# Row maxima of an attention kernel: one shared tile for a pair of heads, one scores tile per unit of work

## The chip, the cores and the metric

The kernel runs on one core of a Trainium2 chip. The metric is the device time of one launch in microseconds, as a median of runs. The core has a matrix engine (TensorE, PE in the profile), a vector engine (VectorE, DVE), a scalar engine (ScalarE, ACT), a general engine (GpSimd, POOL), and a synchronising engine (SyncE, SP) that here issues nearly all DMAs. Each engine works through its own instruction list in order and waits on semaphores for the others.

## The reference

Attention with a threshold, followed by two feed-forward layers. Per batch (4) and head (8), with 576 rows and a head size of 64, in float32:

```python
scores = scale * q @ k.T
thresh = max(scores, axis=-1) - tau
scores = where(scores >= thresh, scores, -1e9)
attn = exp(scores - max(scores)); attn /= sum(attn) + 1e-9
x = attn @ v                       # -> 2304 x 512
x = g(x @ w_in) @ w_out            # 512 -> 2048 -> 512, g piecewise quadratic
x = layernorm(solu(x @ w_in2)) * g_ln @ w_out2   # 512 -> 1024 -> 512
```

The change lies in the attention alone.

## The kernel before

Attention runs over 16 pairs of heads. A pair has nine units of work (`UNITS`), 144 in all. A unit covers 128 keys of one head, except the pair's fifth: 576 is four and a half times 128, so it covers the last 64 keys of the even head and the first 64 of the odd one. For these the keys of the even head lie in columns 0 to 575 of its tiles and those of the odd head in columns 64 to 639 (`key_off`), with zeros in the other 64 columns, so that both heads add up in one tile of scores.

A unit makes the scores with keys on the partitions and queries along the columns, already shifted by the row maximum (`shifted`, tile zt, line 378); ScalarE takes the exponential (`expo`, line 389); VectorE sets to zero what is below the threshold (`mask`, line 394). One unit later `p_split` makes a rounded high half on ScalarE (phi, line 402) and the remainder on GpSimd (plo, line 403), because the matrix engine works in a shortened float32 and each product is made of a high and a low part. Three units later `values` multiplies by v (tile av, line 426), and `store_head` copies a finished head out (xs, line 438).

The shift must be known before a head's first unit. So `scores` makes a head's scores once more ahead of time, with queries on the partitions (tile sc, line 305): five tiles a head, the fifth with only 64 rows in use. `row_max` reduces each (mcol, line 318, VectorE). `row_shift` (ScalarE and GpSimd) turns the five columns into a shift in two parts, `shift_turn` transposes it on TensorE (tile tm, line 339), and `shift_store` copies it (mt, line 345) and writes it by a DMA issued from ScalarE into two rows of q_m (line 346), which the shifted scores read. All this is done once per head.

Before that, `load_kq` loads q and k of a pair by eight DMAs, `transpose_kq` turns them (tr, line 262), `split_kq` makes high (q_st, line 270) and low (lo, line 271) parts, and `stack_k` and `stack_q` copy pieces between partitions by DMA: k_both from q_st (line 285) and from lo (286), q_m from q_st (289), q_st from lo (293). The last one overwrites the rows that the first one reads. SyncE issues all of these, and also the loads of v, the stores of finished heads (lines 440, 441) and the raw weights.

The order on each engine is written by hand. `attention_unit(u)` goes through a string `ORDER[u % 9]`, one letter after another: S one tile of scores, x one row maximum, F the splitting of q and k, E shifted scores and exponential, M mask, v and V the values matmuls, p the split of unit u-1, L the store of a head, P transposes on TensorE, A row shift, shift store and split of v, T the SyncE work, J a step of the weight decoding. The constants give the unit, counted from the pair's first, at which a thing is done: `T_A`, `T_B` the transposes of the even and odd head (stacking one and three units later, the load five units before `T_A`), `S_UNITS` the ten scores tiles, `TURN_AT` the transpose of the shift, `V_AT` the split of v. `T_FIRST`, `T_SECOND` are those of the first two pairs, and `U0` the first unit. Scores, shifted scores and both kinds of transposes share three PSUM buffers (`ps_r`) in the order in which they are issued.

During attention twelve blocks of weights are decoded from 64-bit words by `Jobs`, a new one every `JOB_EVERY` units; `DECODE` says in which unit which kind of step may be done. A step's five VectorE operations are in lines 487 to 500.

## Time and profile before

| | us |
|---|---|
| median of 3 runs (lowest, highest) | 1044.88 (1042.83, 1046.16) |
| the profiled execution's own time | 1043.3 |
| its span, first to last instruction | 1041.5 |
| TensorE busy | 969.5 (93%) |
| VectorE busy | 732.1 (70%) |
| GpSimd busy | 598.0 (57%) |
| ScalarE busy | 535.3 (51%) |

The busy share of TensorE counts a matmul from its start to its modelled end, and successive matmuls overlap; 93% is therefore not a share of its peak. Attention takes about the first 405 us, and the two feed-forward layers the rest.

### The profile page before, as it was taken

How to read it: one execution, taken by the hardware profiler on the slowest of the kernel's cores; microseconds unless marked ns; L12 is line 12 of the kernel's file. 1: busy time of each engine (PE TensorE's matmuls, PEld its weight loads, DVE VectorE, ACT ScalarE, POOL GpSimd, SP SyncE). 2: the span in 40 equal slices, each digit the busy share in tenths (PEclk: the TensorE clock that was granted, in tenths of full speed). 3: DMA queues.
4: the chain of work that ended last, by engine and by line, in shares of the span. 5: the costliest groups of instructions: out<-in, count | busy, mean ns of one | idle time of the engine just before them, and what ended most of it. 6: DMA issues, size and time to landing. Idle time of an engine off the chain costs nothing.

```text
span 1041.5 us, 15175 instructions
## 1 busy us (share of the span) xinstructions
PE 969.5 (93%) x5232; PEld 841.7 (81%) x5232; DVE 732.1 (70%) x1133; ACT 535.3 (51%) x1006; POOL 598.0 (57%) x569
## 2 busy tenths in 40 slices
PE   4899899889979998999999999999999999999998
PEld 3788888788878897767887888788888988888886
DVE  3788888868877775588747875787567556666662
ACT  2666666756756666645443443444344534344433
POOL 6577778967786776657524552555256823344332
PEclk9999999989999999999999999999999999999999
DMA  6555556555755520321121112111211104444443
GB/s 155 136 136 135 124 136 160 136 122 131 184 145 126 132 70 24 91 84 59 33 71 61 42 41 81 51 51 41 91 41 51 56 7 132 108 121 127 122 131 91
DMA packets 89885, 99.89 MB, mean 96 GB/s; under 512 B 50032, under 2 KB 62640, under 8 KB 89808
## 3 DMA queue, kind: packets, MB, share of 16 engines
q1 hardware_dynamic: 89424, 98.76, 36.5%
q8 instruction: 41, 0.67, 0.3%
q14 instruction: 36, 0.29, 0.1%
q10 hardware_dynamic: 384, 0.16, 0.1%
HBM read 55.13 MB, written 15.88 MB: 68 GB/s over the span
## 4 chain that ended last, share of the span: by engine, by line
PE 54%; issue 13%; DVE 12%; POOL 10%; ACT 6%; DMA 3%; SPq 2%; ACTq 0%; POOLq 0%; DVEq 0%
PE y L779 10%; PE h L742 10%; PE o L932 10%; PE h L821 9%; PE av L426 6%; PE zt L378 5%; PE sc L305 3%; DVE e L394 3%; POOL gl L763 3%; POOL dec_a L504 2%; POOL plo L403 2%; POOL wg L533 2%; ACT e L389 2%; DVE mcol L318 2%; DMA q_st<-lo 1%
## 5 line engine op out<-in xcount | busy, mean ns | idle before, releaser
L403 POOL TENSOR_TENSOR plo<-e,phi 128x576 fp32r<-128x576 f32 x144 | 206.2, 1438 | 80.7 <-ACT phi L402 79.5
L763 POOL TENSOR_TENSOR gl<-cl,gh 128x512 fp32r<-128x512 f32 (+1 forms) x80 | 96.9, 1211 | 189.4 <-ACT gh L762 156.0
L779 PE MATMUL y<-gh,wg 128*128 128x512 f32 (+1 forms) x640 | 187.6, 374 | 4.1 <-ACT gh L762 4.1
L742 PE MATMUL h<-xh,wg 128*128 128x512 f32 (+1 forms) x640 | 185.8, 371 | 2.0 <-DVE e L394 2.0
L394 DVE SCALAR_TENSOR_TENSOR e<-zt,ntau,e 128x576 f32<-128x576 f32 x144 | 116.6, 810 | 64.9 <-ACT e L389 64.7
L758 ACT ACTIVATE h<-h,mone 128x512 f32<-128x512 f32 (+1 forms) x80 | 49.5, 619 | 198.8 <-DVE cl L757 198.6
L389 ACT ACTIVATE e<-zt 128x576 f32<-128x576 f32 x144 | 93.7, 651 | 96.6 <-PE zt L378 81.1
L779 PEld LDWEIGHTS y<-gh,wg 128*128 128x128 f32 x640 | 117.9, 188 | 24.1 <-ACT gh L762 7.8
L742 PEld LDWEIGHTS h<-xh,wg 128*128 128x128 f32 x640 | 119.0, 189 | 19.2 <-DVE e L394 2.3
L779 PE MATMUL y<-gl,wg 128*128 128x512 f32 (+1 forms) x320 | 122.0, 381 | 10.2 <-POOL gl L763 10.2
L318 DVE TENSOR_REDUCE mcol<-sc 128x1 f32<-128x576 f32 x160 | 116.7, 747 | 10.4 <-PE sc L305 10.4
L757 DVE TENSOR_SCALAR cl<-h 128x512 f32<-128x512 f32 (+1 forms) x80 | 50.8, 635 | 102.0 <-PE h L742 69.0
L742 PE MATMUL h<-xl,wg 128*128 128x512 f32 (+1 forms) x320 | 118.8, 371 | 0.0
L932 PE MATMUL o<-wg,ln 128*128 128x512 f32 x432 | 103.2, 395 | 0.0
L821 PE MATMUL h<-wg,y 128*128 128x512 f32 x432 | 101.2, 390 | 0.0
L402 ACT CAST phi<-e 128x576 fp32r<-128x576 f32 x144 | 96.3, 669 | 2.1 <-DVE e L394 1.9
L932 PEld LDWEIGHTS o<-wg,ln 128*128 128x128 f32 x432 | 81.0, 188 | 19.2
L821 PEld LDWEIGHTS h<-wg,y 128*128 128x128 f32 x432 | 81.0, 188 | 17.0
L896 POOL TENSOR_TENSOR ln<-land,ln 128x1024 fp32r<-128x1024 f32 x16 | 38.5, 2408 | 92.2 <-ACT ln L895 86.4
L378 PE MATMUL zt<-q_st,k_both 128*128 128x288 f32 x320 | 76.9, 322 | 10.4 <-ACT mt L345 5.2
L305 PE MATMUL sc<-k_both,q_st 128*128 128x288 f32 x320 | 73.4, 312 | 13.1 <-DMA q_st<-lo 8.7
L779 PEld LDWEIGHTS y<-gl,wg 128*128 128x128 f32 x320 | 60.1, 188 | 27.3 <-POOL gl L763 19.1
(109 smaller groups left out, 1940.4 us busy)
## 6 DMA issues: line engine op xcount, KB each, us to landing
raw<-in_moe_w_in_dram SPq DMA_DIRECT2D x24, 512.0 KB
raw<-in_moe_w_out_dram SPq DMA_DIRECT2D x24, 512.0 KB
k_both<-q_st SPq DMA_DIRECT2D x30, 288.0 KB
sq<-so SPq DMA_DIRECT2D x64, 128.0 KB
land<-sq SPq DMA_DIRECT2D x16, 512.0 KB
k_both<-lo SPq DMA_DIRECT2D x32, 144.0 KB
q_st<-lo SPq DMA_DIRECT2D x32, 144.0 KB
x<-xs SPq DMA_DIRECT2D x32, 144.0 KB
```

Source lines behind the costliest of these rows:

```text
L305: nc.tensor.matmul(ps[:, c, 0:HS], lhsT=st[j][i][r, n * P : n * P + P], rhs=kk[j][i][r, o + c * HS : o + (c + 1) * HS], start=(st is q_st) ...
L318: nc.vector.tensor_reduce(mc[:, n : n + 1], sc_ps.pop((h, n))[:, :, 0:HS], axis=AXES.XY, op=ALU.max, negate=True)
L378: nc.tensor.matmul(ps[:, c, 0:HS], lhsT=st, rhs=mv[:, c * HS : (c + 1) * HS], start=(m == 0), stop=(m == len(todo) - 1),)
L389: nc.scalar.activation(out=e, in_=st_ps[u][:, :, 0:HS], func=ACTF.Exp)
L394: nc.vector.scalar_tensor_tensor(out=e, in0=st_ps.pop(u)[:, :, 0:HS], scalar=ntau[:, 0:1], in1=e, op0=ALU.is_ge, op1=ALU.mult)
L402: nc.scalar.copy(hi, e)
L403: (nc.vector if u - NU in LO_DVE or u < NU - UNITS and u % UNITS in LO_UNITS else nc.gpsimd).tensor_tensor(lo, e, f32(hi), op=ALU.subtract)
L742: nc.tensor.matmul(ps, lhsT=a[:, kk, f], rhs=m[:, kk, :], start=(n == 0 and kk == 0), stop=(n == 2 and kk == KD - 1),)
L763: nc.gpsimd.tensor_tensor(gl, cl, f32(gh), op=ALU.subtract)
L779: nc.tensor.matmul(y_ps[c][d], lhsT=a[:, jj, ds_], rhs=m, start=(jj == 0 and n == 0), stop=(jj == JG - 1 and n == 2),)
L821: nc.tensor.matmul(ps[g], lhsT=a[:, kk, :], rhs=wg_t["in2", g][s][:, kk, :], start=(n < 2), stop=(n >= 6 * KD - 2),)
L932: nc.tensor.matmul(ps, lhsT=a[:, f, :], rhs=wg_t["out2", f // 4][m][:, f % 4, :], start=(n == 0), stop=(n == len(terms) - 1))
```

## The change

The odd head's queries now lie in columns 64 to 639 of q_st and q_m, as its keys do, so the fifth scores tile of a pair holds the last 64 queries of the even head and the first 64 of the odd one, with eight matmuls that add up in one tile. A pair has nine scores tiles instead of ten, in the order 0, 1, 2, 3, 5, 4, 6, 7, 8, one per unit from unit -14 to unit -6. The column of maxima of the shared tile is copied once on GpSimd, since both heads need it. Row shift, transpose and copy are done once for the pair (for the first pair still once per head); the two DMAs into q_m remain. One string gives the order of every unit. The transposes stand 6 units earlier (with the loads, five units before), the odd heads' tiles have three buffers instead of two, jobs come every 10 units, v is split at unit -2, and the tiles e, phi, plo, xs and mt each have one buffer fewer.

```diff
-    T_A, T_B = -16, -10
-    S_UNITS = (-10, -9, -7, -7, -6, -5, -4, -3, -3, -2)
+    T_A, T_B = -22, -16
+    S_FIRST = -14
...
-    JOB_EVERY = 9
...
-    ORDER = (
-        "FESvSxvMxxpVPLTASJ",
-        "vFEvSSTSxxMxxxpLVPAJ",
-        "EvvvSSSMxxxVLFPATpJ",
-        "FESvSSxxMxxpVLPATJ",
-        "FESSSMJvxxxpVLPAT",
-        "FEvvSSSMxxxpVLPATJ",
-        "FvJEvSSSMxxxpVLPAT",
-        "FEvvvSSSMxxxVLPvATpJ",
-        "FSEvPSSTMxxxpVLAJ",
-    )
+    JOB_EVERY = 10
...
+    ORDER = "SxFEvMvpVLPATJ"
...
-    V_AT = -5
+    V_AT = -2
...
-    LO_UNITS = ()
...
-    LO_DVE = ()
...
-    T_SECOND = (-13, -2)
+    T_SECOND = (-13, -7)
...
-    DECODE = ('', '', 's', 'asb', '', 's', '', 'as', 'asb')
+    DECODE = ('asb', 's', 'asb', 'a', 'sb', 'asb', 'a', 's', 'asb')
...
-    NBUF = (3, 2)
+    NBUF = (3, 3)
...
     def key_off(h):
...
+    def on(h):
+        return slice(64 * (h % 2), 64 * (h % 2) + S)
...
     def buf(h):
...
-                nc.gpsimd.memset(f32(q_st[j][i][:, S:SP]), 0.0)
-                nc.gpsimd.memset(f32(q_m[j][i][0:D, S:SP]), 0.0)
+                nc.gpsimd.memset(f32(q_st[j][i][:, pad]), 0.0)
+                nc.gpsimd.memset(f32(q_m[j][i][0:D, pad]), 0.0)
...
         for t in v_nat if first else ():
...
-        hi = q_st[j][i][:, 0:S]
+        hi = q_st[j][i][:, on(h)]
...
     def stack_k(h):
...
-        kh = f32(q_st[j][i][0:D, 0:S])
-        o = slice(key_off(h), key_off(h) + S)
+        o = on(h)
+        kh, qh = f32(q_st[j][i][0:D, o]), f32(q_st[j][i][D:P, o])
...
-            nc.scalar.copy(q_m[j][i][0:D, 0:S], f32(q_st[j][i][D:P, 0:S]))
+            nc.scalar.copy(q_m[j][i][0:D, o], qh)
...
-        if h < FAST:
-            return
-        nc.sync.dma_start(f32(q_m[j][i][0:D, 0:S]), f32(q_st[j][i][D:P, 0:S]))
+        if h >= FAST:
+            nc.sync.dma_start(f32(q_m[j][i][0:D, o]), qh)
...
     def stack_q(h):
...
-        nc.sync.dma_start(f32(q_st[j][i][0:D, 0:S]), f32(tr_t.pop(h)[D:P, :]))
+        nc.sync.dma_start(f32(q_st[j][i][0:D, on(h)]), f32(tr_t.pop(h)[D:P, :]))
...
-    def scores(h, n):
-        j, i = buf(h)
-        o = key_off(h)
...
+    S_ORDER = (0, 1, 2, 3, 5, 4, 6, 7, 8)
...
+    def scores(p, n):
...
-        for st, kk in ((q_st, k_st), (q_m, k_on)):
-            r = slice(0, P if st is q_st else R1)
+        todo = []
+        for h in ([2 * p] if n <= 4 else []) + ([2 * p + 1] if n >= 4 else []):
+            j, i = buf(h)
+            at_ = slice((n - 4 * j) * P, (n - 4 * j) * P + P)
+            for st, kk, r in ((q_st, k_st, P), (q_m, k_on, R1)):
+                todo.append((st[j][i][0:r, at_], kk[j][i][0:r, on(h)]))
+        for m, (st, mv) in enumerate(todo):
             for c in range(2):
...
-                    lhsT=st[j][i][r, n * P : n * P + P],
-                    rhs=kk[j][i][r, o + c * HS : o + (c + 1) * HS],
-                    start=(st is q_st),
-                    stop=(st is q_m),
+                    lhsT=st,
+                    rhs=mv[:, c * HS : (c + 1) * HS],
+                    start=(m == 0),
+                    stop=(m == len(todo) - 1),
...
-        sc_ps[h, n] = ps
...
-    def row_max(h, n):
-        if n == 0:
-            mcol[h] = att_p.tile([P, NTI], F32, tag="mcol", name="mcol", bufs=2)
-        mc = mcol[h]
+        sc_ps[p, n] = ps
...
+    def row_max(p, n):
+        if p not in mcol:
+            mcol[p] = att_p.tile([P, 2, NTI], F32, tag="mcol", name="mcol", bufs=2)
+        mc = mcol[p].rearrange("p j n -> p (j n)")
+        m = n + (n > 4)
...
-            mc[:, n : n + 1], sc_ps.pop((h, n))[:, :, 0:HS], axis=AXES.XY, op=ALU.max, negate=True
+            mc[:, m : m + 1], sc_ps.pop((p, n))[:, :, 0:HS], axis=AXES.XY, op=ALU.max, negate=True
...
-    def row_shift(h):
-        mc = mcol.pop(h)
...
-        sh = att_p.tile([P, 2, NTI], F32, tag="sh", name="sh", bufs=2)
-        mr = att_p.tile([P, 2, NTI], F32R, tag="mr", name="mr", bufs=2)
-        nc.scalar.activation(out=sh[:, 0, :], in_=mc, func=ACTF.Abs, scale=DELTA)
-        nc.scalar.activation(out=sh[:, 1, :], in_=sh[:, 0, :], func=ACTF.Relu, bias=ntau[:, 0:1], scale=1.0)
-        nc.gpsimd.tensor_tensor(sh[:, 0, :], sh[:, 1, :], mc, op=ALU.add)
-        nc.gpsimd.tensor_copy(mr[:, 0, :], sh[:, 0, :])
-        nc.gpsimd.tensor_tensor(mr[:, 1, :], sh[:, 0, :], f32(mr[:, 0, :]), op=ALU.subtract)
-        mr_t[h] = mr
+        if n == 4:
+            nc.gpsimd.tensor_copy(mc[:, 5:6], mc[:, 4:5])
...
-    def shift_turn(h):
+    def row_shift(p, js):
...
+        mc = mcol[p][:, js, :]
...
+        sh = att_p.tile([P, 2, 2, NTI], F32, tag="sh", name="sh", bufs=2)
+        mr = att_p.tile([P, 2, 2, NTI], F32R, tag="mr", name="mr", bufs=2)
+        s0, s1, m0, m1 = sh[:, 0, js], sh[:, 1, js], mr[:, js, 0, :], mr[:, js, 1, :]
+        nc.scalar.activation(out=s0, in_=mc, func=ACTF.Abs, scale=DELTA)
+        nc.scalar.activation(out=s1, in_=s0, func=ACTF.Relu, bias=ntau[:, 0:1], scale=1.0)
+        nc.gpsimd.tensor_tensor(s0, s1, mc, op=ALU.add)
+        nc.gpsimd.tensor_copy(m0, s0)
+        nc.gpsimd.tensor_tensor(m1, s0, f32(m0), op=ALU.subtract)
+        mr_t[p, js.start] = mr[:, js]
...
+    def shift_turn(p, js):
...
-        nc.tensor.transpose(ps[0 : 2 * NTI, 0:P], f32(mr_t.pop(h)).rearrange("p l n -> p (l n)"), ident)
-        mr_t[h] = ps
...
-    def shift_store(h):
-        j, i = buf(h)
-        mt = att_p.tile([2 * NTI, P], F32R, tag="mt", name="mt", bufs=2)
-        nc.scalar.copy(mt, mr_t.pop(h)[0 : 2 * NTI, 0:P])
-        nc.scalar.dma_start(f32(q_m[j][i][R1:R3, :]), f32(mt))
+        mr = f32(mr_t.pop((p, js.start))).rearrange("p j l n -> p (j l n)")
+        nc.tensor.transpose(ps[0 : mr.shape[1], 0:P], mr, ident)
+        mr_t[p, js.start] = ps[0 : mr.shape[1], 0:P]
...
+    def shift_store(p, js):
+        mt = att_p.tile([4 * NTI, P], F32R, tag="mt", name="mt", bufs=1)
+        ps = mr_t.pop((p, js.start))
+        nc.scalar.copy(mt[0 : ps.shape[0]], ps)
+        for n, h in enumerate(range(2 * p + js.start, 2 * p + js.stop)):
+            j, i = buf(h)
+            nc.scalar.dma_start(f32(q_m[j][i][R1:R3, :]), f32(mt[2 * NTI * n : 2 * NTI * n + 2 * NTI, :]))
...
-            todo += [(k_st[j][i][:, cols], q_st[j][i]), (k_on[j][i][:, cols], q_m[j][i])]
+            todo += [(k_st[j][i][:, cols], q_st[j][i][:, on(h)]), (k_on[j][i][:, cols], q_m[j][i][:, on(h)])]
         for m, (st, mv) in enumerate(todo):
             for c in range(2):
...
     def expo(u):
-        e = att_p.tile([P, 2, HS], F32, tag="e", name="e", bufs=4)
+        e = att_p.tile([P, 2, HS], F32, tag="e", name="e", bufs=3)
...
     def p_split(u):
...
-        hi = att_p.tile([P, 2, HS], F32R, tag="phi", name="phi", bufs=5)
-        lo = att_p.tile([P, 2, HS], F32R, tag="plo", name="plo", bufs=5)
+        hi = att_p.tile([P, 2, HS], F32R, tag="phi", name="phi", bufs=4)
+        lo = att_p.tile([P, 2, HS], F32R, tag="plo", name="plo", bufs=4)
...
-        (nc.vector if u - NU in LO_DVE or u < NU - UNITS and u % UNITS in LO_UNITS else nc.gpsimd).tensor_tensor(lo, e, f32(hi), op=ALU.subtract)
+        nc.gpsimd.tensor_tensor(lo, e, f32(hi), op=ALU.subtract)
...
     def store_head(h):
...
-            xs = att_p.tile([P, 2, HS], F32, tag="xs", name="xs", bufs=2)
+            xs = att_p.tile([P, 2, HS], F32, tag="xs", name="xs", bufs=1)
...
     for p in range(NP):
-        for n, d in enumerate(S_UNITS):
-            at(s_at, UNITS * p + d, None, 2 * p + n // NTI, n % NTI)
-        for j in range(2):
-            t = UNITS * p + S_UNITS[NTI * j + NTI - 1]
-            at(act_, t + 1, row_shift, 2 * p + j)
-            at(pe_, t + TURN_AT, shift_turn, 2 * p + j)
-            at(act_, t + TURN_AT, shift_store, 2 * p + j)
+        for k_, n in enumerate(S_ORDER):
+            at(s_at, UNITS * p + S_FIRST + k_, None, p, n)
+        for js, last in ((slice(0, 1), 4), (slice(1, 2), 8)) if p == 0 else ((slice(0, 2), 8),):
+            t = UNITS * p + S_FIRST + S_ORDER.index(last)
+            at(act_, t + 1, row_shift, p, js)
+            at(pe_, t + TURN_AT, shift_turn, p, js)
+            at(act_, t + TURN_AT, shift_store, p, js)
...
     def attention_unit(u):
...
         for w, j in ((u - LAGV - 1, 1), (u - LAGV, 0), (u - LAGV, 1)):
...
-        for what in ORDER[u % UNITS]:
+        for what in ORDER:
...
```

## Rows read from the trace of the kernel before

**Rows 1.** Busy time by window: length, each engine (instructions), granted clock, DMA.

```profile
147.30:171.40 24.10, 21.95 (x153) 20.15 (x154) 21.17 (x29) 16.28 (x31) 18.63 (x19) 1.00 0.62 154
195.40:225.00 29.60, 24.37 (x153) 22.28 (x153) 19.69 (x27) 16.52 (x31) 21.40 (x21) 0.88 0.63 155
296.70:325.10 28.40, 23.30 (x153) 21.49 (x152) 19.78 (x27) 16.00 (x30) 19.87 (x20) 0.94 0.65 156
347.90:370.30 22.40, 21.17 (x154) 19.98 (x153) 16.57 (x24) 15.20 (x29) 15.37 (x16) 1.00 0.47 108
```

**Rows 2.** Instruction groups 110 to 330 us, VectorE: busy us, mean ns.

```profile
L318 DVE TENSOR_REDUCE mcol<-sc 128x1 f32<-128x576 f32 x87 | 63.5, 745 | 7.8 <-PE sc L305 7.8
...
L271 DVE SCALAR_TENSOR_TENSOR lo<-tr,scale,q_st 128x576 fp32r<-128x576 f32 x17 | 13.7, 805 | 0.0
L493 DVE SCALAR_TENSOR_TENSOR dec_a<-raw,dec_a 128x512 uint32<-128x512 uint32 x9 | 12.7, 1411 | 0.0
L490 DVE TENSOR_SCALAR dec_a<-dec_a 128x512 uint32<-128x512 uint32 x9 | 12.5, 1390 | 0.0
...
L487 DVE TENSOR_SCALAR dec_a<-dec_a 128x512 f32<-128x512 f32 x9 | 8.5, 949 | 0.0
...
L500 DVE SCALAR_TENSOR_TENSOR raw<-raw 128x512 f32<-128x512 uint32 x9 | 8.2, 911 | 0.0
...
L497 DVE TENSOR_SCALAR raw<-dec_a 128x512 uint32<-128x512 uint32 x8 | 6.6, 827 | 0.0
```

**Rows 3.** Timeline around 163 us: start, length, instruction, idle before.

```profile
163.09 0.43 PE L305 MATMUL sc<-k_both,q_m 65*128 65x288 f32 x2
...
163.36 0.43 PE L426 MATMUL av<-plo,v_hi 128*128 128x288 f32 x2
...
164.52 0.27 PE L339 MATMUL tm<-ident,mr 128*10 128x128 f32 x1 [0.73 <-DVE e L394]
164.83 0.26 ACT L345 CAST mt<-tm 10x128 fp32r<-10x128 f32 x1 [1.40 <-PE tm L339]
...
165.13 0.52 PE L378 MATMUL zt<-q_st,k_both 128*128 128x288 f32 x2 [0.34 <-ACT mt L345]
```

**Rows 4.** Timeline around 152 us, ScalarE and its DMA queue.

```profile
151.82 0.62 ACTq L346 DMA_DIRECT2D q_m<-mt  x1
...
152.54 0.65 ACT L389 ACTIVATE e<-zt 128x576 f32<-128x576 f32 x1 [0.75 <-PE av L426]
```

**Rows 5.** Chain of waits in the two stalls and at the start: start, length.

```profile
199.83 6.12 DMA k_both<-q_st
...
205.97 3.76 DMA q_st<-lo
...
301.38 5.58 DMA k_both<-q_st
...
15.47 2.73 DMA q_st<-lo
```

**Rows 6.** Timeline of the start, TensorE, SyncE and ScalarE.

```profile
13.35 1.38 PE L262 MATMUL tr<-ident,nat 128*128 128x128 f32 x5 [3.90 <-DMA nat<-in_k_dram]
...
18.33 0.82 PE L305 MATMUL sc<-k_both,q_st 128*128 128x288 f32 x2 [3.60 <-DMA q_st<-lo]
...
23.84 1.26 SPq L219 DMA_DIRECT2D nat<-in_q_dram  x2
...
27.79 1.25 SPq L229 DMA_DIRECT2D nat<-in_k_dram  x2
...
29.13 0.64 SPq L285 DMA_DIRECT2D k_both<-q_st  x1
...
29.63 0.65 ACT L389 ACTIVATE e<-zt 128x576 f32<-128x576 f32 x1 [0.48 <-PE zt L378]
```

**Rows 7.** Instruction groups 147.3 to 171.4 us, GpSimd.

```profile
L403 POOL TENSOR_TENSOR plo<-e,phi 128x576 fp32r<-128x576 f32 x10 | 14.2, 1422 | 4.5 <-ACT phi L402 4.5
L253 POOL TENSOR_TENSOR v_lo<-v_nat,v_hi 128x640 fp32r<-128x640 f32 x1 | 1.6, 1579 | 0.0
```

## The prediction

> **What bounds the kernel now.** I read the busy table by stage first. Attention fills the first 405 us or so, and the change touches nothing after it. In a steady stretch of 24.1 us, TensorE (PE) has 153 matmuls and is busy 21.95 us, VectorE (DVE) 21.17, GpSimd (POOL) 18.63 and ScalarE (ACT) 16.28 [rows 1]. One pair of heads needs 152 matmuls (40 of scores, 40 of shifted scores, 60 of values, 10 transposes of q and k, 2 of row maxima), so 24.1 us is the price of a pair while weights are being decoded; after the decoding it is 22.4 us. No engine is full, so next I read the timeline. Two matmuls of 288 columns follow two others after 0.27 us [rows 3]: 0.134 us each, or 20.4 us for 152. The other 3.7 us of a pair are holes, and one hole is in these rows: the last values matmul is issued by 163.63, the transpose of the maxima waits for a score buffer until 164.52, ScalarE copies it out from 164.83, and the next shifted scores start at 165.13. That is 1.5 us. Three buffers of PSUM circulate among scores, shifted scores and transposes, so a tile waits for the third before it to be released.
>
> The third view is the chain of waits. Two stretches carry one pair's matmuls but take 29.6 and 28.4 us instead of 24.1, with the granted clock down to 0.88 and 0.94 [rows 1]. In the first the chain runs through two DMAs in a row: the stacking copy of the k half from 199.83, which takes 6.12 us, and then the copy of the q remainder, 3.76 us [rows 5]. The second may not be issued before the first is through, because it overwrites what the first reads. TensorE can't begin the odd head's scores before both have landed. The second stretch shows the same copy, 5.58 us long.
>
> **The change part by part.**
> *The middle tile.* Per pair the scores are 8 tiles of four matmuls and one of eight: 40 matmuls, as before. TensorE gains nothing but one small transpose of the maxima, 0.27 us of latency and about 0.13 of issue. VectorE loses one reduction of 0.745 us per pair [rows 2]. The row shift runs once instead of twice (two short ScalarE and three short GpSimd instructions fewer, one short GpSimd copy more); it is off the path because both engines have over 5 us free per pair [rows 1].
>
> *The jobs.* A weight block has five VectorE steps: 0.949 + 1.390 + 1.411 + 0.827 + 0.911 = 5.49 us [rows 2]. One per 10 units instead of 9 takes 0.55 us from a pair, and the jobs last 11 units longer, which returns it; I count it at zero. VectorE's load per pair is then 21.17 - 0.75 - 0.55 = 19.9 us, just under TensorE's 20.3.
>
> *One order for all units.* This should set the pace. A unit now has one scores tile, then one shifted tile; before, some units issue two scores tiles together, with the transpose of the maxima right behind them and ahead of the shifted scores. With one scores tile ahead of every shifted tile, the transpose (letter P, at the end of the unit) takes the buffer of the shifted tile of the unit before, whose mask is long done. So the 1.5 us hole goes. The holes at the transposes of q and k I leave: the shifted tile after one still takes the buffer of the last shifted tile. The gain is bounded by 0 (new holes of the same size) and by 24.1 - 20.5 = 3.6 us a pair (a full TensorE). I take the row that I can see, 1.5 us, for the 13 pairs that run with scores all along: -19.5 us.
>
> *Earlier transposes and a third buffer for odd heads.* From a head's stacking to its first scores there were five units for an even head and four for an odd one (from -15 to -10, from -9 to -5); now there are seven and six (from -21 to -14, from -15 to -9). At 2.5 us a unit the odd head's 10 us become 15. The chain that stalled took 199.83 to 209.73, 9.9 us [rows 5], so 15 us covers it. The stalls go: (29.6 - 24.1) + (28.4 - 24.1) = 9.8 us. Next late is SyncE's queue, which issues all of these copies in order. Bounds: 0, if a queue that falls behind uses up the lead, to -9.8. I take -9.8, because the lead grows by more than the 4 us hole.
>
> *The start.* Here the change costs, since moved instructions move past each other on SyncE's queue. Before, head 3 (the odd head of the second pair) is transposed 2 units before unit 0, and the load of q and k for the third pair stands 3 units before it: SyncE issues that load from 23.84 to 29.04, 5.2 us, then head 3's stacking at 29.13; the first exponential is at 29.63 and doesn't need head 3 [rows 6]. Now head 3's first scores are in unit -1, ahead of the first shifted tile on TensorE, and the load (unit -9) and the load of v for pair 1 (unit -7) are ahead of head 3's stacking (unit -6). Worked through: the first scores start at 18.33 as before, for their copies are issued as before. Head 2's transpose, at 13.35 before [rows 6], now follows two score tiles. At half clock these take about 1.1 us each and the transpose 1.4, so it ends near 21.9. With ScalarE's split (under 1 us), the k copy of at least 2.7 us that must be through before the q copy may go, and up to 1 us in the queue, the q copy of head 2 is issued near 26.5. Then 5.2 us of q and k loads and three loads of v at 0.6 each lead to 33.5; head 3's k copy with 2.7 us or more, to 37; its q copy with 2.73 to 3.76 us [rows 5, 6], to 40 or 41. Unit -1's tile, unit 0's double tile and the shifted tile are 16 matmuls: 2.1 us at full clock, about 4.3 at half, as the engine has then been idle. The first exponential comes near 44 instead of 29.6: +14.4. Against it stands work done ahead: five scores tiles and a transpose with its split more than before, on VectorE 5 x 0.745 + 0.805 = 4.5 us [rows 2]. Net +9.9. The bounds are 0 (the copies catch up while other work lasts) and +16 (the k copy as slow as 6.1 us).
>
> On the DMA's length the Trainium skill ("DMA: Bandwidth & Descriptors", section "Anatomy of one DMA") fits about 2.0 us plus bytes over 436 GB/s, for DMAs that GpSimd issues. For the k copy's 288 KB that gives an estimate of 2.7 us, where the trace has 6.12 and 5.58 in the stalls [rows 5]; these are issued by SyncE, among other loads. By the page alone the start would come out 1 to 2 us earlier than I have it, and the old stalls would not exist, so the measurement decides.
>
> *ScalarE and fewer buffers.* A DMA issued from ScalarE holds it: the exponential at 152.54 begins 0.1 us after the issue of 0.62 us that began at 151.82 [rows 4], and the releaser that its row names, a values matmul, is not its input. Both issues of a pair now come back to back in one unit, so an exponential starts some 0.6 us later. One fewer buffer for exponentials, for both halves of the probabilities and for the stored head leaves GpSimd less room to lag. Bounds 0 to 1.6 us a pair (one remainder of v, 1.579 [rows 7], no longer hidden). GpSimd has 5.5 us of 24.1 free, so I take the low side, 0.3 x 15 = +4.5.
>
> Sum: -19.5 - 9.8 + 9.9 + 4.5 = -14.9 us. The profiled execution took 1043.3 us (span 1041.5), so 1028.4; the median of the runs, 1044.88, is 1.6 above it, so I predict 1030.
>
> **The rivals.**
> 1. *GpSimd's ring sets the pace* (slower). With three buffers the exponential of unit u+3 waits until GpSimd has read unit u's. GpSimd takes 1.42 us per unit in any case, and a remainder of v (1.579) and two steps of a job in neighbouring units put it over 4 us behind [rows 7]; ScalarE then stops, in order, and all behind it. For: rows 7 and the in-order queues. Against: GpSimd waits 4.5 us in this stretch for its inputs. At 1.6 us a pair the saved hole is gone and 0.3 us is lost in 13 pairs: 1044.9 - 9.8 + 9.9 + 3.9 = 1049. With everything of a pair counted in, slower begins where a pair costs more than 24.3 us: the stalls and the start then cancel, and 13 x 0.24 is 3.1 us.
> 2. *Only the removed work is saved.* New holes replace the old ones but for a reduction: -0.75 x 13 = -9.7, with the other terms 1039.8. For: the latency of a shifted tile (exponential and mask, over 1.5 us) is as long as before. Against: rows 3.
> 3. *Start cheap, TensorE nearly full.* First exponential near 36 (+2 net) and a pair at 21.8 us (-2.3 x 13 = -30): with -9.8 and +4.5, 1012. For: VectorE and TensorE both come to 20 us. Against: the order of the loads on SyncE.
> 4. *It doesn't take the stalls away*: SyncE lags by more than the added lead, because its loads are earlier too. Then -19.5 + 9.9 + 4.5 + some 4 of lateness elsewhere: 1044, no change. For: GpSimd's normalisation holds a load of reciprocals on SyncE at the ends of batches, where the two stalls lie.
>
> **How the numbers follow.** Forecast 0.42, rivals in order 0.19, 0.20, 0.11, 0.08. This kernel can tell 0.3%, or 3.1 us, from no change: faster is under 1041.8 and slower is over 1048. The forecast lies wholly in faster but for 0.02 in no change; of rival 2, 0.15 is faster and 0.05 none; rival 3 is faster. Rival 1 gives 0.17 slower and 0.02 none; rival 4 gives 0.02 faster, 0.03 none and 0.03 slower. Together 0.68, 0.12, 0.20. The range leaves out about a tenth on each side: 1015 (most of rival 3 outside) to 1048 (the far half of rival 1 outside).
>
> **What would show it.** Right: exponentials of one unit in successive pairs 22.6 us apart while jobs run; no wait of TensorE for the copy of a q remainder after 60 us; the first exponential between 40 and 46; 144 reductions instead of 160, 17 transposes of maxima instead of 32. Wrong: ScalarE's exponentials waiting for GpSimd by more than 1 us per pair (rival 1); VectorE idle for TensorE in every unit at an unchanged 24 us (rival 2); head 3's scores before 34 us (rival 3).

## The result, and the profile after

The kernel became slower: 1053.62 us in the median of 4 runs (1053.03 to 1054.09) against 1043.86 us for the kernel before on the same chip (1041.70 to 1046.16). The ratio is 1.0087, with an interval of 1.0070 to 1.0104. The prediction was 1030 us with a range of 1015 to 1048: the sign and the range were both missed.

The first part of the page of the changed kernel says little: each engine with its busy time, share of the span (1051.2 us) and instructions.

```profile
PE 973.3 (93%) x5217; PEld 843.6 (80%) x5217; DVE 739.2 (70%) x1117; ACT 522.8 (50%) x961; POOL 595.7 (57%) x547
```

One number in it is odd. VectorE (DVE) has 16 instructions fewer than before (1133) and is busy 7.1 us longer (732.1 before).

The second view is the busy time by window, with the columns of [rows 1] (TensorE, its weight loads, VectorE, ScalarE, GpSimd): a steady pair while weights are decoded, and the longest pair.

```profile
116.40:140.70 24.30, 21.67 (x154) 20.03 (x153) 20.49 (x26) 15.34 (x29) 17.93 (x17) 1.00 0.56 133
214.10:239.80 25.70, 22.33 (x153) 20.13 (x152) 21.97 (x26) 15.08 (x27) 19.72 (x19) 1.00 0.58 141
```

A steady pair costs about what it cost before, 24.1 us [rows 1], with the same 152 or so matmuls. The two stalls of 29.6 and 28.4 us [rows 1] are gone; no pair is above 25.7 us. A pair is counted from the first exponential of its first unit to that of the next pair. The profiled executions give this account, which closes:

| part of the span | before | after | difference | predicted |
|---|---|---|---|---|
| up to the first exponential | 29.63 | 46.04 | +16.4 | +14.4 |
| pairs 1 to 13: the two stalls' excess | 9.9 | 0 | -9.9 | -9.8 |
| pairs 1 to 13: the rest | 308.7 | 314.7 | +6.0 | -19.5 pace, +4.5 ScalarE and buffers, -4.5 work ahead |
| pairs 0, 14, 15, and all behind attention | | | -2.8 | 0 |
| span | 1041.5 | 1051.2 | +9.7 | -14.9 |

The third line is the failure. The view that opens it is VectorE's groups of instructions by line from 46 to 380 us (busy us, mean ns, idle before), which answers to [rows 2]:

```profile
L315 DVE TENSOR_REDUCE mcol<-sc 128x1 f32<-128x576 f32 x125 | 93.4, 748 | 9.1 <-PE sc L301 8.9
...
L504 DVE SCALAR_TENSOR_TENSOR raw<-raw 128x512 f32<-128x512 uint32 x12 | 20.1, 1678 | 0.0
L491 DVE TENSOR_SCALAR dec_a<-dec_a 128x512 f32<-128x512 f32 x12 | 17.3, 1444 | 0.0
L497 DVE SCALAR_TENSOR_TENSOR dec_a<-raw,dec_a 128x512 uint32<-128x512 uint32 x12 | 14.9, 1244 | 0.0
L501 DVE TENSOR_SCALAR raw<-dec_a 128x512 uint32<-128x512 uint32 x12 | 14.0, 1165 | 0.0
L494 DVE TENSOR_SCALAR dec_a<-dec_a 128x512 uint32<-128x512 uint32 x12 | 10.6, 886 | 0.0
```

The row maxima take 748 ns, as before (745). The five steps of a block of weights, untouched by the change, now take 1.678 + 1.444 + 1.244 + 1.165 + 0.886 = 6.42 us, where [rows 2] have 5.49 (5.53 when counted from 30 to 330 us). The timeline shows how (start, length, instruction, idle before):

```profile
312.25 0.82 DVE L398 SCALAR_TENSOR_TENSOR e<-zt,ntau,e 128x576 f32<-128x576 f32 x1 [0.52 <-ACT e L393]
...
312.37 0.43 PE L301 MATMUL sc<-k_both,q_m 65*128 65x288 f32 x2
...
312.91 1.43 POOL L407 TENSOR_TENSOR plo<-e,phi 128x576 fp32r<-128x576 f32 x1 [0.46 <-POOL mcol L319]
312.98 1.64 DVE L501 TENSOR_SCALAR raw<-dec_a 128x512 uint32<-128x512 uint32 x1
...
314.54 0.74 DVE L315 TENSOR_REDUCE mcol<-sc 128x1 f32<-128x576 f32 x1
...
315.34 0.53 PE L382 MATMUL zt<-q_st,k_both 128*128 128x288 f32 x2 [0.69 <-DVE mcol L315]
...
360.70 1.43 POOL L407 TENSOR_TENSOR plo<-e,phi 128x576 fp32r<-128x576 f32 x1 [0.55 <-POOL mcol L319]
360.78 1.39 DVE L457 TENSOR_SCALAR sm<-sm 128x36 f32<-128x36 f32 x1
...
362.50 0.63 DVE L497 SCALAR_TENSOR_TENSOR dec_a<-raw,dec_a 128x512 uint32<-128x512 uint32 x1
362.50 1.89 POOL L407 TENSOR_TENSOR plo<-e,phi 128x576 fp32r<-128x576 f32 x1 [0.38 <-ACT phi L406]
...
364.43 0.42 DVE L501 TENSOR_SCALAR raw<-dec_a 128x512 uint32<-128x512 uint32 x1
```

The reader is to compare the two rows of line 501. At 364.43 the operation takes 0.42 us, with no GpSimd instruction beside it. At 312.98 it takes 1.64 us: GpSimd's remainder (plo) had begun 0.07 us earlier and ran to 314.34, and the VectorE step ended 0.28 us behind it. So three quarters of its "busy" time is lengthening, not work. An operation on 36 columns (360.78) takes 1.39 us in the same way. Where the two begin together (362.50), GpSimd is the one that lengthens, from 1.43 to 1.89 us.

This is no accident of one unit. In the uniform order the step (J) stands right behind the mask (M). The mask ends 0.82 us after the exponential, and plo begins after phi, which takes 0.66 us: here the step comes a tenth of a microsecond too late. Of the 60 steps between 46 and 400 us, 58 stand right behind a mask, 53 begin while a GpSimd operation of over 1 us is running, and 42 take over 1 us themselves. What it delays is in the same rows. The scores of the next head were through at 312.80; their row maximum starts at 314.54, behind the step; the shifted scores at 315.34 take the buffer that this row maximum frees. Where TensorE stood still, in total us, times and longest, from 92 to 336 us, is the waits view:

```profile
PE sc L301 <- DVE mcol L315: 9.1, 15, 0.9
PE zt L382 <- DVE mcol L315: 7.5, 9, 1.4
PE av L430 <- ACT xs L442: 3.9, 5, 1.2
...
PE tm L341 <- DVE mcol L315: 0.6, 2, 0.3
```

In the kernel before, over four steady pairs (99 to 195.5 us), no row of the same view names the row maxima; it has these three among others:

```profile
PE tm L339 <- DVE e L394: 2.4, 4, 0.8
...
PE tr L262 <- DVE e L394: 2.1, 4, 0.5
PE zt L378 <- ACT mt L345: 1.4, 4, 0.3
```

The hole of [rows 3] (tm behind a mask, then zt behind mt) did go: 3.8 us in four pairs, 0.95 us a pair. The wait of the transposes of q and k (tr) went too, 0.5 us a pair. Waits for row maxima, 17.2 us in ten pairs or 1.7 us a pair, stand in their place.

The start is in the chain of waits (start, length), beside SyncE's queue and the first exponential, which answer to [rows 6]. First the queue and ScalarE:

```profile
26.36 1.29 SPq L210 DMA_DIRECT2D nat<-in_q_dram  x2
...
30.35 1.25 SPq L220 DMA_DIRECT2D nat<-in_k_dram  x2
...
34.71 1.10 SPq L236 DMA_DIRECT2D v_nat<-in_v_dram  x2
35.91 0.64 SPq L276 DMA_DIRECT2D k_both<-q_st  x1
...
46.04 0.65 ACT L393 ACTIVATE e<-zt 128x576 f32<-128x576 f32 x1 [7.45 <-PE zt L382]
```

Then the chain:

```profile
35.91 3.42 DMA k_both<-q_st
...
39.34 2.35 DMA q_st<-lo
...
41.83 3.22 PE sc L301 x12
```

Head 3's copy of k is issued at 35.91 behind the loads of pair 2 and of v, lands after 3.42 us, lets the copy of q go, and the first exponential follows 4.2 us after the scores can start. The last row has 12 matmuls in 3.22 us, 0.27 us each or twice the 0.134 of a steady pair, though the granted clock of the profile reads 1.00 there (40 to 46 us).

### The profile page after: what moved, and what is told of

Same layout as the page of the kernel before. It is cut to its first block, busy times and chain, and to the rows that moved or that the text cites. A ratio compares the mean times of both kernels' runs of the same rounds, so it can differ in the third digit from the quotient of the medians.

```text
span 1051.2 us, 14953 instructions
## 1 busy us (share of the span) xinstructions
PE 973.3 (93%) x5217; PEld 843.6 (80%) x5217; DVE 739.2 (70%) x1117; ACT 522.8 (50%) x961; POOL 595.7 (57%) x547
## 4 chain that ended last, share of the span: by engine, by line
PE 53%; DVE 16%; issue 13%; POOL 8%; ACT 6%; SPq 2%; DMA 2%; ACTq 1%; POOLq 0%; DVEq 0%
PE y L784 10%; PE o L937 10%; PE h L747 9%; PE h L826 9%; PE sc L301 5%; PE zt L382 5%; PE av L430 4%; DVE e L398 3%; DVE mcol L315 3%; POOL gl L768 3%; ACT e L393 2%; POOL wg L537 2%; POOL dec_a L508 1%; DVE raw L501 1%; DVE dec_a L491 1%
## 5 line engine op out<-in xcount | busy, mean ns | idle before, releaser
L407 POOL TENSOR_TENSOR plo<-e,phi 128x576 fp32r<-128x576 f32 x144 | 211.4, 1470 | 90.1 <-ACT phi L406 79.5
L784 PEld LDWEIGHTS y<-gh,wg 128*128 128x128 f32 x640 | 117.9, 188 | 24.1 <-ACT gh L767 7.8
L315 DVE TENSOR_REDUCE mcol<-sc 128x1 f32<-128x576 f32 x144 | 107.8, 748 | 31.4 <-PE sc L301 31.2
L301 PE MATMUL sc<-k_both,q_st 128*128 128x288 f32 x320 | 79.9, 333 | 28.5 <-DMA q_st<-lo 12.2
L301 PEld LDWEIGHTS sc<-k_both,q_st 128*128 128x128 f32 x320 | 54.2, 204 | 39.2 <-DVE mcol L315 16.0
L382 PE MATMUL zt<-q_st,k_both 128*128 128x288 f32 x320 | 73.3, 311 | 12.0 <-DVE mcol L315 11.3
```

The lines of the kernel that those rows point to most:

```text
L301: nc.tensor.matmul(ps[:, c, 0:HS], lhsT=st, rhs=mv[:, c * HS : (c + 1) * HS], start=(m == 0), stop=(m == len(todo) - 1),)
L315: nc.vector.tensor_reduce(mc[:, m : m + 1], sc_ps.pop((p, n))[:, :, 0:HS], axis=AXES.XY, op=ALU.max, negate=True)
L382: nc.tensor.matmul(ps[:, c, 0:HS], lhsT=st, rhs=mv[:, c * HS : (c + 1) * HS], start=(m == 0), stop=(m == len(todo) - 1),)
L407: nc.gpsimd.tensor_tensor(lo, e, f32(hi), op=ALU.subtract)
L784: nc.tensor.matmul(y_ps[c][d], lhsT=a[:, jj, ds_], rhs=m, start=(jj == 0 and n == 0), stop=(jj == JG - 1 and n == 2),)
```

## The experiments

The theory: **the place of the decode step decides**. A step on VectorE and plo on GpSimd exclude each other, and right behind the mask the step nearly always comes second. The rivals: the decoding costs time wherever it stands; any VectorE work at the end of a unit does it, whatever its kind; it is not the decoding at all, but the start and the fewer buffers. Each ratio is against the kernel before, run beside it (medians 1044.56, 1043.52 and 1044.76 us in the three groups of runs).

**1 and 2. Both kernels without decoding inside attention** (the blocks are decoded behind it). Labels a_nojobs (changed kernel) and b_nojobs (kernel before):

```
-    JOBS_FROM = -1
+    JOBS_FROM = 1000
...
     scores_ps.close()
+    jobs.finish()
```

> The changed kernel with no weight decoding during attention (all blocks are decoded after it, so only the pace of attention is read from this run). Theory P, the decode step at the end of a unit holds the next row maximum back: a pair of heads takes 21 to 21.8 us instead of 24.1, and TensorE's waits for row maxima, some 1.7 us a pair, nearly go. Rival L, one scores tile ahead of each shifted tile is slow by itself with three score buffers: a pair still takes 23 us or more.

> The kernel before with no weight decoding during attention, as the pair to the other run without decoding. Both theories: 22.4 us a pair, as in its own pairs after the decoding. Theory P wants the changed kernel below this by 0.6 us or more; rival L wants it level or above.

Measured: 1087.92 and 1085.68 us, one run each; the decoding behind attention adds to both. What is compared is one pair, at a granted clock of 1.00 in both, in the windows of the first and of the second kernel:

```profile
112.10:133.60 21.50, 20.89 (x152) 19.88 (x151) 14.95 (x21) 14.42 (x27) 14.96 (x15) 1.00 0.56 125
```

```profile
96.00:118.40 22.40, 21.16 (x155) 19.97 (x154) 15.56 (x22) 15.22 (x30) 15.32 (x17) 1.00 0.54 120
```

A pair takes 21.5 us against 22.4. Over pairs 1 to 13 it is 283.0 us against 295.2, so the uniform order, with its fewer buffers, saves 12.2 us, 0.9 a pair. With decoding the same pairs take 314.7 and 308.7 us (the latter without the stalls' excess): the decoding costs the uniform order 31.7 us and the order before 13.5. That difference of 18.2 turns the saving into the +6.0 of the account. The start has no part in that, and the fewer buffers by themselves none either, as this kernel has them too.

What the order saves without decoding shows in TensorE's waits of the kernel before (b_nojobs, 95 to 330 us, some ten pairs):

```profile
PE tr L262 <- DVE e L394: 7.6, 10, 1.0
PE zt L378 <- ACT mt L345: 3.4, 10, 0.3
...
PE tm L339 <- DVE e L394: 0.2, 1, 0.2
```

The same view of a_nojobs has none of the three. Most of it is the wait of the transposes of q and k, which the prediction had left in place; the hole of [rows 3] is 0.36 us a pair here.

**3. The step ahead of the shifted scores** (a_jx):

```
-    ORDER = "SxFEvMvpVLPATJ"
+    ORDER = "SxFJEvMvpVLPAT"
```

> The changed kernel with the decode step (letter J) moved from the end of the unit to between the row maximum and the shifted scores. Theory P: the five VectorE operations of a block fall from 6.42 us in sum to 5 or less, since GpSimd's subtraction then runs at another time, a pair takes about 22.5 us, and the time is about 1034. Rival L: a pair stays at 24 us and the time at 1053.

Measured: 1034.8 us (1033.01 to 1040.56), ratio 0.9924 [0.9895, 0.9953]. One letter is worth 1.6% of the time. VectorE's groups from 46 to 380 us and the windows of this kernel, in a profiled execution of 1040.56 us, the upper end of that range:

```profile
L497 DVE SCALAR_TENSOR_TENSOR dec_a<-raw,dec_a 128x512 uint32<-128x512 uint32 x12 | 14.0, 1168 | 0.0
L491 DVE TENSOR_SCALAR dec_a<-dec_a 128x512 f32<-128x512 f32 x12 | 12.5, 1044 | 0.0
```

```profile
89.50:111.90 22.40, 21.44 (x153) 19.98 (x151) 18.51 (x25) 15.30 (x29) 18.12 (x17) 1.00 0.63 142
205.00:231.70 26.70, 24.18 (x153) 22.58 (x151) 20.23 (x26) 15.62 (x28) 21.41 (x19) 0.87 0.57 136
```

With 987, 904 and 833 ns for the other three, a block's steps take 4.94 us instead of 6.42, and most pairs 21.9 to 22.4. Four pairs in the middle stay slow (23.9 to 26.8 us; the granted clock is 1.00 in the first and between 0.87 and 0.93 in the other three). The timeline of the longest shows a step of 1.89 us, begun 0.07 us behind a GpSimd operation of 1.41 us (the normalisation of a finished batch), in a unit that also has a transpose of q and k; the mask and then TensorE wait for it:

```profile
210.16 1.41 POOL L477 TENSOR_TENSOR x<-x,rb 128x576 f32<-128x576 f32 x1
...
210.23 1.89 DVE L497 SCALAR_TENSOR_TENSOR dec_a<-raw,dec_a 128x512 uint32<-128x512 uint32 x1
...
212.05 0.80 DVE L398 SCALAR_TENSOR_TENSOR e<-zt,ntau,e 128x576 f32<-128x576 f32 x1
...
212.91 0.85 PE L382 MATMUL zt<-q_st,k_both 128*128 128x288 f32 x2 [1.62 <-DVE e L398]
```

The pair loses more than the wait. In slices of 2 us the granted clock is 1.00 up to 212 us, 0.50 from 214 to 218 (the lower level, 1.2 GHz) and 1.00 again from 220; before it fell, TensorE was busy for 1.29 us of the slice from 210. In this pair TensorE is busy for 24.18 us with the matmuls that take 21.44 in the other window.

**4. Head 3's transpose earlier, the next loads and transposes later** (a_start), against the cost of the start:

```
-    T_SECOND = (-13, -7)
+    T_SECOND = (-13, -10)
...
+    LATE = {2: 4, 3: 3, 4: 2, 5: 1}
...
-            t = (T_FIRST, T_SECOND)[p][j] if p < 2 else UNITS * p + (T_A, T_B)[j]
+            t = (T_FIRST, T_SECOND)[p][j] if p < 2 else UNITS * p + (T_A, T_B)[j] + LATE.get(p, 0)
...
-            at(late_, UNITS * p + T_A - 5, load_kq, p)
+            at(late_, UNITS * p + T_A - 5 + LATE.get(p, 0), load_kq, p)
```

> The changed kernel with head 3's transpose three units earlier, and the loads and transposes of pairs 2 to 5 later by 4, 3, 2 and 1 units, so that on SyncE head 3's copies go ahead of the third pair's load. If the order on SyncE makes the late start: the first exponential comes at 36 to 38 us instead of 46, and the time is 1045 to 1049 (a part is given back where the third pair's copies are now late). Rival: the start only moves a wait, and the time stays at 1052 or more.

Measured: 1071.66 us, ratio 1.0272 [1.0245, 1.0299], a miss. The first exponential did come earlier, at 39.58 instead of 46.04 (expected 36 to 38), but pairs 0 to 2 took 38.6, 28.1 and 30.0 us. TensorE's waits from 39 to 110 us name the copies of the pairs made later (the copy of the q remainder has another 4.2 us):

```profile
PE sc L301 <- DMA k_both<-lo: 7.4, 2, 7.0
```

The wait moved behind the first exponential and grew.

**5. Decode steps of a kind that doesn't contend** (a_nolock). The five VectorE steps of the blocks decoded in attention become reductions of the same 128x512 tile to one column, in the same places; the kernel leaves these weights undecoded, so only its pace is read:

```
+    def red(a):
+        nc.vector.tensor_reduce(warm, a, axis=AXES.X, op=ALU.max)
...
-        nc.vector.tensor_scalar(a, a, MAG_LOW, MAG_HIGH, op0=ALU.max, op1=ALU.min)
+        if fine[0]:
+            red(a)
+        else:
+            nc.vector.tensor_scalar(a, a, MAG_LOW, MAG_HIGH, op0=ALU.max, op1=ALU.min)
...
```

> The changed kernel with the five VectorE operations of a decoded block each replaced, during attention, by a maximum along the same 128x512 tile into one column (the weights of these blocks are then not decoded; the pace is what is read). Such a step has one SBUF input and about 0.6 us, so a block keeps about 3 us of VectorE work at the same places. Theory P1, the steps are stretched because they and GpSimd's subtraction exclude each other: no step is stretched, a pair takes 21.7 to 22.3 us, the time is about 1029. Theory P2, any step at the end of a unit holds the next row maximum back: a pair stays above 23.3 us and the time above 1043.

Measured: 1023.29 us (1022.34 to 1025.58), ratio 0.981 [0.9787, 0.9834], by the ratios some 29 us under the changed kernel. The group of these steps from 46 to 380 us:

```profile
L484 DVE TENSOR_REDUCE warm<-dec_a 128x1 f32<-128x512 f32 x60 | 40.5, 675 | 0.0
```

As in the changed kernel, 58 of the 60 steps stand right behind a mask, and 51 begin while a GpSimd operation of over 1 us is running; none is drawn out: 675 ns each (628 to 679). A step that is longer than the undisturbed 0.42 us costs less: pairs 1 to 13 take 288.2 us, 26.5 less than in the changed kernel, out of the 31.7 that the whole decoding cost them. It is the exclusion and not the place as such: "any VectorE work at the end of a unit" falls. The Trainium skill ("SBUF — State Buffer", section "Who interferes with whom") has it so: VectorE's second port pair is shared with GpSimd under an exclusive lock, the first to issue keeps it for its whole instruction, and a reduction never needs it. By that rule the steps of one tensor input in a fast mode and those of two inputs are blocked and the reductions are not; the rows of lines 501 and 484 agree. That the former run in a fast mode no view shows; 0.41 us alone, against 0.68 for a reduction of the same tile, fits it.

**6. The start again, with only pair 2 later** (a_start2): as 4, but `LATE = {2: 2}`.

> The changed kernel with head 3's transpose three units earlier and only the third pair's load and transposes two units later, so that SyncE issues head 3's copies ahead of that load and the later pairs stay as they are. If the order on SyncE makes the late start: the first exponential at about 41 us instead of 46, no new waits in the first three pairs, time 1047 to 1050. Rival: what the start gains is lost in the first pairs again, time 1052 or more.

Measured: 1060.83 us, ratio 1.0171 [1.015, 1.0192], a miss. Head 3's copy of q was issued at 31.23, 8.1 us earlier, but the first exponential came at 45.88, no earlier: TensorE's transposes of pair 2 now stand just ahead of it and wait 3.6 us for their load. Pair 0 took 32.7 us; TensorE's scores wait 6.4 us in it for the copy of a q remainder. SyncE's queue:

```profile
45.73 1.28 SPq L210 DMA_DIRECT2D nat<-in_q_dram  x2
...
49.71 1.25 SPq L220 DMA_DIRECT2D nat<-in_k_dram  x2
51.00 0.59 SPq L283 DMA_DIRECT2D q_st<-lo  x1
```

The load of the next pair (45.73 to 50.96) now stood ahead of another copy. In both runs that moved the load later on SyncE, the first pairs waited for a copy.

**7. Only a longer lead, in the kernel before** (b_lead): two units instead of six, the third buffer for odd heads, and the fewer buffers for e, phi, plo, xs and mt that pay for it (these lines are left out here):

```
-    T_A, T_B = -16, -10
+    T_A, T_B = -18, -12
...
-    NBUF = (3, 2)
+    NBUF = (3, 3)
```

> The kernel before with one part of the change alone: transposes two units earlier, a third buffer for odd heads, and, to make room, the fewer buffers for e, phi, plo, xs and mt of the change. If the two stalls come from a short lead of the stacking copies: no pair over 26 us, and the time 1033 to 1037. Rival: the strings, written for other places of the transposes, or the fewer buffers cost as much, and the time stays at 1042 or more.

Measured: 1036.8 us (1035.28 to 1041.08), ratio 0.9941 [0.9921, 0.9962]. The windows of two of its pairs, in the stretches where [rows 1] have 29.6 and 28.4 us:

```profile
197.50:221.70 24.20, 22.34 (x155) 20.19 (x154) 20.48 (x27) 16.24 (x32) 21.40 (x21) 1.00 0.55 140
293.90:317.50 23.60, 22.07 (x154) 20.08 (x153) 19.74 (x27) 15.75 (x30) 19.89 (x20) 1.00 0.67 178
```

No pair is above 24.5 us, and the clock of 0.88 and 0.94 is gone with the stalls. This part of the prediction holds by itself. Pairs 1 to 13 take 311.2 us, 2.5 more than the 308.7 of the kernel before without its stalls; so one buffer less for exponentials, probabilities and stored heads can have cost some 2.5 us there, and no more unless something else was gained.

**8. Experiments 3 and 6 together** (a_jx_start2).

> The changed kernel with both: the decode step ahead of the shifted scores, and the start of the other run. If the two causes are independent: 1035 minus 4 to 6, so 1029 to 1031. If the first pairs are bound by something else once the steps are moved: 1034 or more.

Measured: 1043.76 us, ratio 1.001 [0.9993, 1.0026], a miss for the same reason: pair 0 takes 33.1 us. Against a_jx it loses 0.9%.

**9. The load of pair 2 issued from ScalarE** (a_actload), which is idle then:

```
     def load_kq(p):
+        dma = nc.scalar if p == 2 else nc.sync
...
-            nc.sync.dma_start(
+            dma.dma_start(
```

> The changed kernel with the third pair's loads of q and k issued by ScalarE instead of SyncE, at the same place. Theory: the late start is SyncE's issue time; without these 5.2 us ahead of head 3's copies the first exponential comes at 39 to 41 us instead of 46, SyncE is ahead afterwards too, and the time is 1047 to 1049. Rival: the first pairs wait for the copies themselves or for the row maxima, and the time stays at 1052 or more, as when the loads were only moved on SyncE.

Measured: 1048.88 us (1043.1 to 1049.72), ratio 1.0036 [1.0018, 1.0054], against 1.0087 of the changed kernel. SyncE's queue, then ScalarE:

```profile
30.61 0.64 SPq L277 DMA_DIRECT2D k_both<-q_st  x1
```

```profile
40.59 0.65 ACT L394 ACTIVATE e<-zt 128x576 f32<-128x576 f32 x1 [4.63 <-PE zt L383]
```

Head 3's copy of k goes 5.3 us earlier and the first exponential 5.45 us earlier. The same bytes are moved, so it is the place in SyncE's queue, not a lack of bandwidth, that made this part of the start.

**10. The step ahead of the shifted scores, and none on VectorE in the two units with transposes** (a_jx_dec): as 3, and

```
-    DECODE = ('asb', 's', 'asb', 'a', 'sb', 'asb', 'a', 's', 'asb')
+    DECODE = ('asb', 's', 'a', 'a', 'sb', 'a', 'a', 's', 'asb')
```

> The changed kernel with the decode step ahead of the shifted scores and no VectorE step of it in the two units of a pair that transpose q and k (there the shifted scores that follow wait for the last mask, which the step now delays). If that is what is left of the lock's cost: pairs at 21.6 to 22, none above 24, time 1027 to 1031. If not: 1034, as with the moved step alone.

Measured: 1029.64 us (1029.23 to 1030.8), ratio 0.9852 [0.9833, 0.9871]. A block's steps take 4.49 us, and the slow stretch of experiment 3 is gone but for one pair of 25.2 us, which the expectation had ruled out: in it TensorE waits 2.0 us for the copy of a q remainder, and the granted clock is 0.93. A step between a row maximum and the next mask, in the timeline:

```profile
90.64 0.74 DVE L315 TENSOR_REDUCE mcol<-sc 128x1 f32<-128x576 f32 x1
...
91.30 0.41 DVE L501 TENSOR_SCALAR raw<-dec_a 128x512 uint32<-128x512 uint32 x1
...
92.00 0.82 DVE L398 SCALAR_TENSOR_TENSOR e<-zt,ntau,e 128x576 f32<-128x576 f32 x1 [0.29 <-ACT e L393]
```

Here it takes 0.41 us, and the mask is still early: it waits 0.29 us for its exponential. This is one of the shortest of its line, whose twelve in attention have a median of 0.68 us: the other place makes the meeting with GpSimd's operations rarer and shorter, and doesn't end it.

**11. All three** (a_jx_dec_act): the order of 3, the `DECODE` of 10, the load of 9.

> All three: the decode step moved, none in the units with transposes, and the third pair's loads issued by ScalarE. If the parts add up: 5 us below the run without the loads moved, 1022 to 1026. If the start is not SyncE's issue time: the same as that run.

Measured: 1024.71 us (1020.14 to 1028.04), ratio 0.9801 [0.9771, 0.983]; the first exponential is at 42.55, 3.5 us earlier than in experiment 10. It beats the kernel before by 2.0% and the changed one by 2.8% (0.9801 over 1.0087).

## Why the prediction was wrong

**The step that failed is the price of the decode steps: "The jobs", counted at zero, under "One order for all units", -19.5 us.** The prediction took the hole of [rows 3] away, which is right, and left every other duration as it was, which is not: the decode steps were priced at the means of [rows 2], as if a step had a duration of its own. It hasn't: the same operation took 0.41 us alone, 0.96 when it began 0.75 us behind plo, and 1.64 when it began 0.07 us behind it, and the order decides which. In the 13 pairs the decoding cost 18.2 us more in the new order than in the old one (experiments 1 and 2), where the prediction had 0. In place of -19.5, +4.5 and -4.5 the pairs gave +6.0. Moving the letter changed the ratio from 1.0087 to 0.9924, and taking the exclusion out with the letter in its place changed it to 0.981; so the cause is shown from both sides.

**The size of the hole was off too, by less.** The 1.5 us count the instructions in it; TensorE's idle time in these rows is 0.73 + 0.34 = 1.07 us, and 0.95 a pair over four pairs. Without decoding the order with its buffers saves 12.2 us in 13 pairs, where -19.5 and +4.5 make -15; that these are near is in part luck, since most of the saving is the transposes' wait, which the prediction had left in place.

The warning was in the rows that I used. [Rows 2] give 949 and 827 ns for two operations of one kind on tiles of one size, and 1390 for a third; such a spread among means was a sign of something outside the operation, and I added the means up.

**"Earlier transposes and a third buffer for odd heads", -9.8: right.** The stalls gave back 9.9 us, and a lead of two units with its buffers alone brought 6.7 us (experiment 7). The lead itself was misread: tile 5 stands ahead of tile 4, so an odd head's first scores are in unit -10, five units and not six after its stacking; at 2.5 us a unit that is 12.5 us, which still covers the 9.9.

**"The start": the mechanism was right, the size 2.0 us short.** Head 3's copies stand behind the loads, as foreseen: the loads begin at 26.36 (predicted 26.5), the copy of k is issued at 35.91 (33.5, since SyncE stood still from 32.23 to 34.71 ahead of the last loads of v), the copy of q lands at 41.7 (40 or 41). The "half clock" of the 16 matmuls is seen in their pace, 4.2 us for the predicted 4.3, and not in the granted clock. That the work done ahead gives 4.5 us back is not seen: pairs 14 and 15 are shorter by 1.3 us together (33.2 against 34.5 up to the last exponential), and the rest, if there is any, can't be told apart in the +6.0. The prediction's remark that the start would be 1 to 2 us earlier with the shorter estimate for a DMA doesn't follow from its own sum, which has the k copy at 2.7 us already.

**"ScalarE and fewer buffers", +4.5: not told apart.** In the order before, 13 pairs with the fewer buffers took 2.5 us more (experiment 7); without decoding the changed kernel runs a pair in 21.5 us with them and with ScalarE's two issues in it. TensorE's 3.9 us in ten pairs for the store of heads (xs, one buffer now) may be part of it; that was not tested by itself.

**The signs named in advance.** 144 reductions and 17 transposes of maxima: as said. No wait for the copy of a q remainder after 60 us: as said, TensorE has none. First exponential between 40 and 46: 46.04, at the edge. Pairs of 22.6 us: 24.2. "VectorE idle for TensorE in every unit at an unchanged 24 us" was to show rival 2: the 24 us are there and the idleness is not (9.1 us before 125 row maxima), since VectorE was late and not early.

**The rivals.** Rival 1 (GpSimd sets the pace) gave the nearest time, 1049, by luck: its own terms, 1.6 us a pair against a saving of 1.5, make 0.1 us of loss and not 0.3, which gives 1046. It was not the mechanism: exponentials wait for plo 5.2 us in the 216 us from 116 to 332, 0.6 us a pair, where it needed more than 1. The engine was the right one, but it stops VectorE, not ScalarE. Rival 2 (new holes replace the old) described the outcome in the pairs without the cause, and its price, -9.7, was still too good by 16 us, since it kept the steps' length. Rival 4's stalls did not come back.

## What to carry to other kernels

Before a VectorE operation that reads two SBUF tensors or runs in a fast mode is moved, look at which GpSimd instruction begins beside its new place: the price is not the operation's mean but whether it comes first, and a fixed order can lose that race in unit after unit. A busy share doesn't show this, as the wait is counted as work; compare the shortest and the longest of the same operation (0.41 and 1.64 us here). Where a queue in order carries both large loads and small urgent copies, moving the load to an idle engine's queue helped here, and moving it in time, tried in two ways, only changed which copy was waited for.

## What the runs showed of the hardware that was not expected

- The cost of the exclusion goes by what is left of the GpSimd operation and not by size: 36 columns beside plo took 1.39 us, where 1.35 us of plo were left; in the kernel before, two of these took 0.17 us each.
- However late in plo the drawn-out operation of 128x512 began, it ended 0.28 us behind it: begun 0.07, 0.13 and 0.75 us into plo's 1.43, it took 1.64, 1.57 and 0.96 us (the steps of one tensor input). The 0.28 are less than the 0.41 us that it takes alone.
- The same operation on 128x512 took 0.41 us alone and 1.64 us when it began 0.07 us behind plo; a step that began together with plo took 0.63 us, and plo then 1.89 instead of 1.43. Where one of the two had begun, the other paid.
- The eight issues of one load hold SyncE for 5.2 us in the changed kernel (26.36 to 31.60), and moving them to another engine brought the first exponential 5.45 us forward.
